# W casts on GpSimd, sorted x cleared by three engines at the start, batch 1 turned in other PSUM banks

## The chip, the core and the metric

The kernel runs on one core of one Trainium2 chip. The metric is the device time of one execution in microseconds (us): the median of three runs, lower is better. A core has five engines that run side by side[...]: TensorE (PE in the profile, its weight loads as PEld), VectorE (DVE), ScalarE (ACT), GpSimd (POOL) and SyncE (SP), which here issues the loads. Sixteen DMA engines move data between memory and the on-chip buffer.

## What is computed

Eight batches of 576 tokens go through a linear attention with eight heads of width 64. The result is one row of 512 numbers for each of 4608 tokens. It then passes a mixture of experts in which each token goes to one expert:

```python
q_s = softmax(q, axis=-1); k_s = softmax(k, axis=2)      # over the tokens
kv  = einsum('bhsd,bhse->bhde', k_s, v)                  # 64 x 64 per head
x   = einsum('bhsd,bhde->bhse', q_s, kv)                 # -> (4608, 512)

logits = x @ w_gate + modality_bias[modality_id]         # 8 experts, 2 modalities
e_idx  = argmax(logits)
gate_w = softmax(logits)[e_idx]
out[mask_e] = gate_w * (relu(x[mask_e] @ w1[e]) @ w2[e]) # w1: 512 x 1024, w2: 1024 x 512
```

The bias of a modality is large against the rest, so that all tokens of a modality go to one expert. The kernel uses this: it takes two experts from the biases, loads only their weights, and sorts each batch's tokens to the left or to the right end of a buffer `xs`, one expert each. Where the data doesn't fit this picture, a general path at the end computes all experts again. On this draw it is not entered.

## The kernel before

For each batch `attend(b)` computes kv, turns q (`tp_ps`, `et`) and the gate logits; `route(b)` finds each token's expert and its place, computes x (`x_ps`), scales it (`x_sb`), and multiplies it with a permutation, so that tokens come out sorted and turned (`xT_ps`); ScalarE writes them into `xs` twice, left and right. `slots(b)` and `places(b)` build the lists of row numbers by which the results are stored. The FFN is cut into pieces: a piece of the first layer is eight matmuls of 256 columns and a relu into `hT`, one of the second is four matmuls of 512 columns; `mains(n)` issues n pieces. Each function is a generator, and the program order on every engine is the order in which the generators are advanced. A `yield` carries a weight, and `weave` issues pieces in proportion to it.

```python
    stage = ctx.enter_context(tc.tile_pool(name="stage", bufs=6))   # loads of k, v, q, W
    ka = ... bufs=2 (PSUM);  mm = ... bufs=2;  ff = ... bufs=3;  sp_ps = ... bufs=1
    ...
    xs = persist.tile([P, KD, NSLOT], BF16)          # 128 x 4 x 4864
    lst = persist.tile([P, 3, NSL], FP32)
    nc.gpsimd.memset(lst, 0.0)
    xs_w = {}

    def clear(b):
        lo, hi = S * b, min(S * (b + 1), NSLOT // 2)
        xs_w[b] = [
            nc.gpsimd.memset(xs[:, :, c : c + hi - lo].bitcast(FP32), 0.0) for c in (lo, NSLOT - hi)
        ]

    clear(0)
    clear(1)
    ...
    def prep(b, v_eng):          # exp of k and q on ScalarE, cast of v on v_eng
    def attend(b):
        ...
        tps, tag = (ff, "ff") if b == 0 else (mm, "mm")   # banks in which q is turned
        ...
    def x_tile(b, t):
        x_ps = mm.tile([P, 512], FP32, name="x_ps", tag="mm")
    ...
    def route(b):
        ...                      # logits, max, expert: lg, mx, eqm, kk, isa, na, pos on VectorE
        nc.scalar.activation(out=lg, in_=lg, func=ACT.Exp)
        ...
        xps = [x_tile(b, 0)]
        yield 1.6
        xps.append(x_tile(b, 1))
        yield 2.4
        nc.tensor.matmul(out=r_ps[:, 0, :], lhsT=tri, rhs=isa, start=True, stop=True)
        ...                      # gsum, qi, aoff, aoff_i, pos, perm on VectorE
        scale(0)                 # x_sb of tile 0
        yield 5
        scale(1)
        free[0] = nc.vector
        for t in range(NT):      # five tiles of 64 or 128 tokens
            ...                  # xT_ps: four matmuls; x_tile(b, t + 2)
            for side, off in (("a", 0), ("b", right)):
                w = nc.scalar.copy(out=window(a + off, b, T, off > 0), in_=xT_ps[:, :, 0:T])
                if t == 0:
                    after(w, xs_w.pop(b, ()), "tokens come to cleared places")
            yield 1.2 if t < NT - 1 else 1.3
            if t + 2 < NT:
                scale(t + 2)
    ...
    def slots(b):                # VectorE: slot, hi, lo, hhi, hlo;  GpSimd: hv
    def places(b):               # TensorE: id_ps;  VectorE: lst, idb, ab, sel
```

Of the kernel before, what the change touches and what calls it, by code (L numbers as in the profile page):

```python
# [20 lines left out]
P = 128  # L21
# [21 lines left out]
def kernel(  # L43
# [67 lines left out]
    def load_batch(b, names="kvq", halves=""):  # L111
        for nm in names:
            src = {"k": k, "v": v, "q": q}[nm]

            t = stage.tile([P, HG, NJ * Dh], FP32, name="st", tag="st")
            n = HG // 2 if nm in halves else HG
            for g in range(0, HG, n):
                nc.sync.dma_start(
                    out=t[:, g : g + n, :],
                    in_=bass.AP(  # L120
                        tensor=src.tensor,
                        offset=src.offset + (b * H + 2 * g) * S * Dh,
                        ap=[[NJ * Dh, P], [2 * S * Dh, n], [1, NJ * Dh]],
                    ),
                )
            st[nm, b] = t
# [67 lines left out]
    def token_ids():  # L194
        nc.vector.tensor_scalar(out=idh_i, in0=id_i, scalar1=7, scalar2=None, op0=ALU.logical_shift_right)
        nc.vector.tensor_scalar(out=idl_i, in0=id_i, scalar1=127, scalar2=None, op0=ALU.bitwise_and)
        nc.vector.tensor_copy(out=vals[:, :, :, 0], in_=idh_i)
        nc.vector.tensor_copy(out=vals[:, :, :, 1], in_=idl_i)
# [20 lines left out]
    xs = persist.tile([P, KD, NSLOT], BF16)  # L219
    lst = persist.tile([P, 3, NSL], FP32)  # L220
    nc.gpsimd.memset(lst, 0.0)
    xs_w = {}

    def clear(b):

        lo, hi = S * b, min(S * (b + 1), NSLOT // 2)
        xs_w[b] = [
            nc.gpsimd.memset(xs[:, :, c : c + hi - lo].bitcast(FP32), 0.0) for c in (lo, NSLOT - hi)
        ]

    clear(0)
    clear(1)
    aoff_i = persist.tile([1, B * NT], I32)

    krow = persist.tile([P, NSL], FP32)
# [5 lines left out]
    eid_i = const.tile([1, 2], I32)  # L241
    bsel = const.tile([P, B * NT, E], FP32)
    modf = const.tile([P, B, NT], FP32)
    nc.vector.memset(modf, 0.0)

    def gating():

# [59 lines left out]
        nc.vector.tensor_copy(out=view(modf, [[1, NT - 1], [NT, B]], 1), in_=m_ps[:, 1:NT, :])  # L307
        nc.vector.tensor_copy(out=modf[0:64, :, 0], in_=m_ps[0:64, 0, :])

    def bias_of_tokens():  # L310
        biasd = const.tile([P, E], FP32, name="biasd")
        nc.vector.tensor_sub(out=biasd, in0=bias_b[:, 1, :], in1=bias_b[:, 0, :])
        nc.vector.tensor_tensor(
            out=bsel, in0=view(modf, [[1, B * NT], [0, E]]), in1=view(biasd, [[0, B * NT], [1, E]]), op=ALU.mult
        )
        nc.vector.tensor_tensor(
            out=bsel, in0=bsel, in1=view(bias_b, [[0, B * NT], [1, E]]), op=ALU.add
        )
# [29 lines left out]
    def after(ins, befores, why):  # L348
        for before in befores:
            tc.add_manual_dep(  # L350
                ins.ins,
                before.ins.name,
                mybir.DependencyInfo(mybir.DependencyClass.Sync, mybir.DependencyReason.DATA),
                reason=why,
            )
# [27 lines left out]
    def attend(b):  # L383

        kvbd, gx, et, vb = kvbd_b[b % 2], gx_b[b % 2], et_b[b % 2], vb_b[b % 2]
        ek, eq = eks[b], eqs[b]
        tps, tag = (ff, "ff") if b == 0 else (mm, "mm")
        kv = [ka.tile([P, 512], FP32, name="kv_ps", tag="ka") for _ in range(2)]
        for hp in range(2):
            for j in range(NJ):  # L390
# [68 lines left out]
        else:  # L459
# [4 lines left out]
                if nj > 1:  # L464
                    yield 1.2 if c0 == 0 else 2
            kvT = kv_turned()
        yield 3
        g_ps = sp_ps.tile([P, NP, E], FP32, name="g_ps", tag="sp")
        for p_ in range(NP):
            nc.tensor.matmul(  # L470
# [67 lines left out]
    def route(b):  # L538
# [38 lines left out]
        def scale(t):  # L577
            T = tsz[t]
            x_out[t] = mid.tile([P, D], BF16, name="x_sb")
            nc.vector.tensor_tensor(  # L580
                out=view(x_out[t], [[2 * Dh, HG], [Dh, 2], [1, Dh]], 0, (0, T)),
                in0=view(xps[t], [[2 * Dh, HG], [Dh, 2], [1, Dh]], 0, (0, T)),
                in1=view(qi, [[1, HG], [HG, 2], [0, Dh]], t * H, (0, T)),
                op=ALU.mult,
            )
# [21 lines left out]
            skip_runtime_bounds_check_because=WHY,  # L607
        )[1]
        scale(0)
        yield 5  # L610
        scale(1)
        free[0] = nc.vector
        for t in range(NT):
            T = tsz[t]
            xT_ps = (ka if b else ff).tile([P, KD, P], FP32, name="xT_ps", tag="ka" if b else "ff")
            for kd in range(KD):
                nc.tensor.matmul(  # L617
                    out=xT_ps[:, kd, 0:T],
                    lhsT=x_out[t][0:T, kd * P : (kd + 1) * P],
                    rhs=perm[0:T, t, 0:T],  # L620
                    start=True,
                    stop=True,
                )
            if t + 2 < NT:
                xps.append(x_tile(b, t + 2))
            right = NSLOT - (b * S + cum[t])
            for side, off in (("a", 0), ("b", right)):
                a = nc.s_assert_within(at[t], 0, b * S + cum[t] - T, skip_runtime_bounds_check_because=WHY)
                w = nc.scalar.copy(out=window(a + off, b, T, off > 0), in_=xT_ps[:, :, 0:T])  # L629
                if t == 0:  # L630
                    after(w, xs_w.pop(b, ()), "tokens come to cleared places")
            yield 1.2 if t < NT - 1 else 1.3
            if t + 2 < NT:
                scale(t + 2)
        free[0] = nc.scalar
# [203 lines left out]
    def alone(*sides):  # L839
        for side in sides:  # L840
            for _ in side:
                pass
# [11 lines left out]
    load_weights(eids[1], 1, nc.sync)  # L854
    for b in range(2, B):
        load_batch(b)
    def steps(side, n):
        for _ in range(n):
            next(side)
# [6 lines left out]
    biases()  # L866
    steps(a0, 2)
    steps(p0, 2)
    bias_of_tokens()
    alone(a0)  # L870
    steps(p1, 2)
# [5 lines left out]
    steps(r0, 1)  # L877
    a1 = attend(1)
    steps(a1, 4)
    token_ids()  # L880
    cast_weights(0, 0, nc.gpsimd)

    for _ in range(NT - 1):
        steps(r0, 1)
        steps(a1, 1)
    alone(r0)
    cast_weights(0, 1, nc.scalar)
    alone(a1)
    mains(1)
    r1 = route(1)  # L890
    cast_weights(0, 2, nc.scalar)
    steps(r1, 1)
    mains(1)
    cast_weights(0, 3, nc.scalar)
    steps(r1, 1)
    mains(2)
    steps(r1, 1)
    slots(0)
    cast_weights(1, 0, nc.gpsimd)
    for b in range(2, 5):  # L900
        clear(b)
    mains(1)
    places(0)
    mains(1)
    weave([next(r1)], 0.6)
    cast_weights(1, 1, nc.vector)
    weave(r1, 0.6)
    cast_weights(1, 2, nc.scalar)
    cast_weights(1, 3, nc.scalar)
    mains(12 - now[0])  # L910
    slots(1)
    p2 = prep(2, nc.gpsimd)
    for i in range(6):
        mains(1)
# [5 lines left out]
    def batch(b):  # L920
        side = chain(attend(b), route(b))
        for i, x in enumerate(side):
            if i == 3 and b > 2:
                slots(b - 1)
            if i == 6 and b > 2:
                places(b - 1)
            yield x

    for b in range(2, B):
        weave(batch(b), (14 if b == 2 else 15.5) / 28.6, prep(b + 1, nc.gpsimd) if b + 1 < B else (), 4)  # L930

    big = persist.tile([1, 2], I32)
    isb = persist.tile([1, 1], FP32)
# [77 lines left out]
    with tc.For_i(0, nr) as e:  # L1011
        kcol = small.tile([P, 1], FP32, name="kcol")
        first = nc.vector.tensor_copy(out=kcol, in_=view(wrow, [[1, 1]], e))
        after(first, stored, "rows are stored again")
        for part in range(4):
            dst = W[:, 0, part * 2 * F : (part + 1) * 2 * F]
            if part < 2:
                nc.gpsimd.dma_start(
                    out=view(dst, [[F, 2], [1, F]]),
                    in_=bass.AP(  # L1020
                        tensor=moe_w1.tensor,
                        offset=e * (D * F) + part * 2 * P * F,
                        ap=[[F, P], [P * F, 2], [1, F]],
                    ),
                )
            else:
                nc.gpsimd.dma_start(
                    out=view(dst, [[D, 4], [1, D]]),
                    in_=bass.AP(
                        tensor=moe_w2.tensor,  # L1030
                        offset=e * (F * D) + (part - 2) * 4 * P * D,
                        ap=[[D, P], [P * D, 4], [1, D]],
                    ),
                )
        sel1 = small.tile([P, NSL], FP32, name="sel1")
        nc.vector.tensor_scalar(out=sel1, in0=lst[:, 2, :], scalar1=kcol, scalar2=None, op0=ALU.is_equal)
        nc.vector.scalar_tensor_tensor(
            out=sel1, in0=idb, scalar=-OOB, in1=sel1, op0=ALU.add, op1=ALU.mult
        )
        for _, _, lo, w in passes:  # L1040
            hT = hbuf.tile([P, KF, GW], BF16, name="hT")
            alone(ffn1(xs[:, :, lo : lo + w], w, weights_of(0)[0], hT))
            alone(ffn2(w, weights_of(0)[1], hT, lambda: rows_of(sel1, lo, w), "stores again"))


# [28 lines left out]
```

The softmax here doesn't subtract the row's maximum and nothing guards it: scores larger than these inputs give would overflow.

## Time and profile before

| what | value |
|---|---|
| median of three runs | 267.23 us (265.94 to 267.35) |
| span of the profiled execution | 265.6 us |
| TensorE busy | 200.6 us, 76% |
| VectorE busy | 151.4 us, 57% |
| ScalarE busy | 153.8 us, 58% |
| GpSimd busy | 78.7 us, 30% |
| read from memory, written | 36.75 MB, 9.70 MB |

A row of the profile's list of stages has the stretch, its length, the busy time of each engine with the number of instructions, the clock granted to TensorE as a share of its full speed, the busy share of the DMA engines, and GB/s. A row of the list of waits reads "engine, what it was about to do, its line <- the engine and the work that ended last before it": total us, times, longest. A row of the timeline has start, duration, engine, line, operation, output <- input with shapes, and how many in a row; neighbours of a kind are merged. The duration on VectorE includes time in which an instruction has been issued and can't run.

### The profile page before, as it was taken

The numbers are of one execution on the slowest core, as the hardware profiler recorded it, in microseconds if no ns is written. First come the engines' busy times: TensorE is split into PE (matmuls) and PEld (weight loads), VectorE is DVE, ScalarE is ACT, GpSimd is POOL, SyncE is SP. The second block draws the span as 40 slices with busy tenths as digits, with TensorE's granted clock in tenths as the row PEclk, the third lists the DMA queues.
The fourth block names the chain that finished last, engine by engine and source line by source line (L and its number), as shares of the span: only waits on it lengthen the run. The fifth ranks groups of instructions, "written<-read, shape, count | busy, mean of one in ns | idle before, by whom it ended". The sixth has DMA issues, their size and how long they took to land. (4 is left out here: it accounts for less than half of the span.)

```text
span 265.6 us, 5231 instructions
## 1 busy us (share of the span) xinstructions
PE 200.6 (76%) x1934; PEld 137.4 (52%) x1954; DVE 151.4 (57%) x501; ACT 153.8 (58%) x241; POOL 78.7 (30%) x94
## 2 busy tenths in 40 slices
PE   0465668447898978898797899888788979999900
PEld 0354545135666447545565575566456637676500
DVE  7488573783043848876793967579385855311110
ACT  2977378138798559666666777665744634443300
POOL 8301000765114216022602341180142052141410
PEclk9995557759799999999999999999999999999975
DMA  6999999566999942861774010210102003030210
GB/s 233 371 390 404 393 391 321 200 206 234 356 389 343 355 174 50 346 237 64 238 246 172 2 79 0 81 79 2 42 12 111 0 39 121 0 158 2 110 57 1
DMA packets 18940, 46.58 MB, mean 175 GB/s; under 512 B 1229, under 2 KB 1229, under 8 KB 18910
## 3 DMA queue, kind: packets, MB, share of 16 engines
q1 hardware_dynamic: 15920, 36.70, 38.9%
q0 software_dynamic: 2960, 9.44, 8.8%
q8 instruction: 17, 0.28, 0.4%
q14 instruction: 13, 0.11, 0.1%
q10 hardware_dynamic: 30, 0.05, 0.1%
HBM read 36.75 MB, written 9.70 MB: 175 GB/s over the span
## 5 line engine op out<-in xcount | busy, mean ns | idle before, releaser
L726 PE MATMUL h_ps<-xs,W 128*128 128x256 bf16 x576 | 74.2, 282 | 4.7 <-ACT hT L737 2.7
L744 PE MATMUL y_ps<-W,hT 128*128 128x512 bf16 x268 | 68.9, 386 | 1.3 <-issue 0.3
L757 POOL DMA_INDIRECT out_dram<-y_sb,ix x37 | 36.7, 991 | 111.9 <-DVE y_sb L358 29.9
L726 PEld LDWEIGHTS <-W 128*128 128x128 bf16 x576 | 55.7, 101 | 14.3 <-issue 3.6
L737 ACT ACTIVATE hT<-h_ps 128x512 bf16<-128x512 f32 x73 | 42.0, 596 | 21.1 <-PE h_ps L726 20.3
L629 ACT CAST xs<-xT_ps 128x512 f32 (+2 forms) x80 | 38.8, 563 | 13.6 <-PE xT_ps L617 13.3
L744 PEld LDWEIGHTS <-hT 128*128 128x128 bf16 x296 | 26.9, 98 | 25.2 <-issue 1.1
L358 ACT COPY y_sb<-y_ps 128x512 f32<-128x512 f32 x22 | 12.9, 586 | 43.2 <-PE y_ps L744 40.9
L580 DVE TENSOR_TENSOR x_sb<-x_ps,qi 128x512 bf16<-128x512 f32 (+1 forms) x40 | 29.8, 764 | 1.2 <-PE x_ps L509 0.5
L358 DVE COPY y_sb<-y_ps 128x512 f32<-128x512 f32 x15 | 10.4, 692 | 33.0 <-PE y_ps L744 33.0
L659 POOL TENSOR_TENSOR hv<-hhi,vals 128x570 bf16<-128x570 bf16 x8 | 12.5, 1568 | 46.3 <-DVE hhi L655 42.5
L617 PE MATMUL xT_ps<-perm,x_sb 128*128 128x128 bf16 (+1 forms) x160 | 16.6, 232 | 9.2 <-DVE x_sb L580 6.6
L617 PEld LDWEIGHTS <-x_sb 128*128 128x128 bf16 (+1 forms) x160 | 10.9, 106 | 19.3 <-DVE x_sb L580 15.2
L376 ACT ACTIVATE ek<-st 128x1152 bf16<-128x1152 f32 x16 | 18.6, 1172 | 1.6 <-DMA st<-in_k_dram 1.6
L376 ACT ACTIVATE eq<-st 128x1152 bf16<-128x1152 f32 x16 | 18.4, 1158 | 0.6 <-DMA st<-in_q_dram 0.6
L509 PE MATMUL x_ps<-kvbd,et 128*128 128x128 bf16 (+1 forms) x160 | 17.5, 239 | 0.4 <-DVE et L358 0.4
L393 PE MATMUL kv_ps<-vb,ek 64*128 64x129 bf16 x288 | 12.8, 239 | 5.9 <-DVE vb L358 2.8
L429 PE MATMUL tp_ps<-ident,eq 128*128 128x128 bf16 x144 | 13.6, 241 | 4.1 <-DVE x_sb L580 2.4
L429 PEld LDWEIGHTS <-eq 128*128 128x128 bf16 x144 | 11.3, 109 | 9.1 <-issue 5.9
L393 PEld LDWEIGHTS <-ek 64*128 64x128 bf16 x288 | 10.3, 104 | 9.7 <-issue 7.6
L358 POOL CAST vb<-st 128x1152 bf16<-128x1152 f32 x12 | 13.5, 1152 | 0.0
L509 PEld LDWEIGHTS <-et 128*128 128x128 bf16 (+1 forms) x160 | 11.8, 109 | 3.3 <-issue 2.2
(148 smaller groups left out, 217.4 us busy)
## 6 DMA issues: line engine op xcount, KB each, us to landing
st<-in_k_dram SPq DMA_DIRECT2D x8, 1152.0 KB, 5.9
st<-in_moe_w_dram SPq DMA_DIRECT2D x8, 1024.0 KB, 12.6
st<-in_v_dram SPq DMA_DIRECT2D x7, 1152.0 KB, 6.3
st<-in_q_dram SPq DMA_DIRECT2D x6, 1152.0 KB, 5.7
st<-in_q_dram SPq DMA_DIRECT2D x4, 576.0 KB, 12.9
st<-in_v_dram SPq DMA_DIRECT2D x2, 576.0 KB, 8.1
out_dram<-y_sb,ix POOLq DMA_INDIRECT x37, 2.8
W<-in_moe_modality_id_dram ACTq DMA_DIRECT2D x1, 36.0 KB
```

Of the source, the lines that this page charges most:

```text
L358: return (nc.scalar.copy if eng is nc.scalar else eng.tensor_copy)(out=out, in_=in_)
L376: nc.scalar.activation(out=view((eks if nm == "k" else eqs)[b], [[Dh, 2], [HG * Dh, NJ], [1, Dh]], 2 * g * Dh), in_=src[:, 2 * g : 2 * g + ...
L393: nc.tensor.matmul(out=kv[hg][:, 130 * hp : 130 * hp + 129], lhsT=ek[rows, j, P * hp : P * hp + P], rhs=vb[rows, j, hp, 0:129], start=(j = ...
L429: nc.tensor.transpose(out=view(tp[c0], [[2 * nj * 64, 2], [1, 64]], hp * nj * 64 + jj * 64), in_=eq[:, c0 + jj, P * hp : P * hp + P], iden ...
L509: nc.tensor.matmul(out=view(x_ps, [[2 * Dh, 2], [1, Dh]], (4 * (p_ % 2) + p_ // 2) * Dh, (0, T)), lhsT=et[:, p_, tcol[t] : tcol[t] + T], r ...
L580: nc.vector.tensor_tensor(out=view(x_out[t], [[2 * Dh, HG], [Dh, 2], [1, Dh]], 0, (0, T)), in0=view(xps[t], [[2 * Dh, HG], [Dh, 2], [1, Dh ...
L617: nc.tensor.matmul(out=xT_ps[:, kd, 0:T], lhsT=x_out[t][0:T, kd * P : (kd + 1) * P], rhs=perm[0:T, t, 0:T], start=True, stop=True,)
L629: w = nc.scalar.copy(out=window(a + off, b, T, off > 0), in_=xT_ps[:, :, 0:T])
L726: nc.tensor.matmul(out=h_ps[:, f * w : (f + 1) * w], lhsT=w1(kd * F + (f0 + f) * P, P), rhs=x_in[:, kd, :], start=(kd == 0), stop=(kd == K ...
L737: nc.scalar.activation(out=h_out, in_=h_in, func=ACT.Relu)
L744: nc.tensor.matmul(out=y_ps, lhsT=hT[:, kf, t * P : (t + 1) * P], rhs=w2(kf * D, D), start=(kf == 0), stop=(kf == KF - 1),)
L757: store = nc.gpsimd.indirect_dma_start(out=out, out_offset=bass.IndirectOffsetOnAxis(ap=ix[:, t : t + 1], axis=0), in_=y_sb, in_offset=Non ...
```

## The change

It moves work between engines and in program order; the matmuls of the main path are the same.

- `xs` is cleared at the start, in four rows of 2432 words of four bytes: two rows on GpSimd, one on ScalarE (as a copy of a zero), one on VectorE. The clears of single batches go, and so do those that ran between batch 0 and batch 2.
- Of the eight parts of W (parts 0 to 3 of the first expert, 4 to 7 of the second), six are cast by GpSimd and two by ScalarE. Before, GpSimd cast two, ScalarE five and VectorE one.
- Batch 1's q is turned in the three FFN banks and no longer in the two banks that it shares with `x_ps`.
- Token ids, `slots(0)`, `slots(1)`, `places` and part of the bias work move in the order; `scale(1)` comes ahead of its yield; some weights differ, and batch 2 is woven with 12 pieces in place of 14.
- The general path becomes a loop over passes inside the loop over experts, in place of a written-out list.

```diff
-    xs_w = {}
-    def clear(b): ...
-    clear(0)
-    clear(1)
+    xs_w = [nc.gpsimd.memset(xs[:, kd, :].bitcast(FP32), 0.0) for kd in (2, 3)]
...
     nc.vector.memset(modf, 0.0)
+    xs_w.append(nc.scalar.copy(out=xs[:, 0, :].bitcast(FP32), in_=view(modf, [[0, NSLOT // 2]])))
...                            # biasd and the product with modf move from bias_of_tokens() to biases()
-        tps, tag = (ff, "ff") if b == 0 else (mm, "mm")
+        tps, tag = (ff, "ff") if b < 2 else (mm, "mm")
...
-        yield 3
+        yield 2.6
         g_ps = sp_ps.tile([P, NP, E], FP32, name="g_ps", tag="sp")
...
         scale(0)
-        yield 5
         scale(1)
+        yield 4.2
...
-                if t == 0:
-                    after(w, xs_w.pop(b, ()), "tokens come to cleared places")
-            yield 1.2 if t < NT - 1 else 1.3
+                if b == 0 and t == 0:
+                    after(w, xs_w, "tokens come to cleared places")
+            yield 1.4 if t < NT - 1 else 2
...
     for b in range(2, B):
         load_batch(b)
+    xs_w.append(nc.vector.memset(xs[:, 1, :].bitcast(FP32), 0.0))
...
     steps(p0, 2)
+    steps(a0, 2)
     bias_of_tokens()
     alone(a0)
...
     a1 = attend(1)
     steps(a1, 4)
+    cast_weights(0, 0, nc.gpsimd)
+    cast_weights(0, 1, nc.gpsimd)
+    steps(r0, 2)
+    ...                        # r0 and a1 in turn
+    alone(r0)
     token_ids()
-    cast_weights(0, 0, nc.gpsimd)
-    for _ in range(NT - 1):
-        steps(r0, 1)
-        steps(a1, 1)
-    alone(r0)
-    cast_weights(0, 1, nc.scalar)
+    slots(0)
+    steps(a1, 1)
     alone(a1)
+    cast_weights(0, 2, nc.scalar)
     mains(1)
     r1 = route(1)
-    cast_weights(0, 2, nc.scalar)
     steps(r1, 1)
-    mains(1)
+    mains(2)
     cast_weights(0, 3, nc.scalar)
     steps(r1, 1)
-    mains(2)
-    steps(r1, 1)
-    slots(0)
-    cast_weights(1, 0, nc.gpsimd)
-    for b in range(2, 5):
-        clear(b)
-    mains(1)
     places(0)
     mains(1)
-    weave([next(r1)], 0.6)
-    cast_weights(1, 1, nc.vector)
-    weave(r1, 0.6)
-    cast_weights(1, 2, nc.scalar)
-    cast_weights(1, 3, nc.scalar)
-    mains(12 - now[0])
+    cast_weights(1, 0, nc.gpsimd)
+    cast_weights(1, 1, nc.gpsimd)
+    steps(r1, 1)
+    mains(2)
+    cast_weights(1, 2, nc.gpsimd)
+    cast_weights(1, 3, nc.gpsimd)
+    weave(r1, 0.8)
     slots(1)
+    mains(14 - now[0])
...
-            if i == 6 and b > 2:
+            if i == 7 and b > 2:
                 places(b - 1)
...
-        weave(batch(b), (14 if b == 2 else 15.5) / 28.6, ...)
+        weave(batch(b), (12 if b == 2 else 15.5) / 28.9, ...)
...                            # general path:
-        for _, _, lo, w in passes:
+        with tc.For_i(0, NSL, GW // P) as at:
+            ...
```

More of the change, by code (lines that the diff above doesn't have):

```diff
@@ L221 @@
     nc.gpsimd.memset(lst, 0.0)
-    xs_w = {}
[L224 to L229, printed above, removed]
-    clear(0)
-    clear(1)
+    xs_w = [nc.gpsimd.memset(xs[:, kd, :].bitcast(FP32), 0.0) for kd in (2, 3)]
     aoff_i = persist.tile([1, B * NT], I32)
@@ L243 @@
     modf = const.tile([P, B, NT], FP32)
+    biasd = const.tile([P, E], FP32)
     nc.vector.memset(modf, 0.0)
+    xs_w.append(nc.scalar.copy(out=xs[:, 0, :].bitcast(FP32), in_=view(modf, [[0, NSLOT // 2]])))
     def gating():
@@ L308, in biases @@
         nc.vector.tensor_copy(out=modf[0:64, :, 0], in_=m_ps[0:64, 0, :])
-    def bias_of_tokens():
-        biasd = const.tile([P, E], FP32, name="biasd")
         nc.vector.tensor_sub(out=biasd, in0=bias_b[:, 1, :], in1=bias_b[:, 0, :])
@@ L315, in bias_of_tokens @@
         )
+    def bias_of_tokens():
         nc.vector.tensor_tensor(
@@ L879 @@
     steps(a1, 4)
-    token_ids()
-    cast_weights(0, 0, nc.gpsimd)
-    for _ in range(NT - 1):
-        steps(r0, 1)
-        steps(a1, 1)
-    alone(r0)
-    cast_weights(0, 1, nc.scalar)
+    cast_weights(0, 0, nc.gpsimd)
+    cast_weights(0, 1, nc.gpsimd)
+    steps(r0, 2)
+    steps(a1, 1)
+    steps(r0, 1)
+    steps(a1, 1)
+    steps(r0, 1)
+    steps(a1, 1)
+    alone(r0)
+    token_ids()
+    slots(0)
+    steps(a1, 1)
     alone(a1)
+    cast_weights(0, 2, nc.scalar)
     mains(1)
     r1 = route(1)
-    cast_weights(0, 2, nc.scalar)
     steps(r1, 1)
-    mains(1)
+    mains(2)
     cast_weights(0, 3, nc.scalar)
     steps(r1, 1)
-    mains(2)
-    steps(r1, 1)
-    slots(0)
-    cast_weights(1, 0, nc.gpsimd)
-    for b in range(2, 5):
-        clear(b)
-    mains(1)
     places(0)
     mains(1)
-    weave([next(r1)], 0.6)
-    cast_weights(1, 1, nc.vector)
-    weave(r1, 0.6)
-    cast_weights(1, 2, nc.scalar)
-    cast_weights(1, 3, nc.scalar)
-    mains(12 - now[0])
+    cast_weights(1, 0, nc.gpsimd)
[5 more added lines that the diff above has]
+    weave(r1, 0.8)
     slots(1)
+    mains(14 - now[0])
     p2 = prep(2, nc.gpsimd)
@@ L929 @@
     for b in range(2, B):
-        weave(batch(b), (14 if b == 2 else 15.5) / 28.6, prep(b + 1, nc.gpsimd) if b + 1 < B else (), 4)
+        weave(batch(b), (12 if b == 2 else 15.5) / 28.9, prep(b + 1, nc.gpsimd) if b + 1 < B else (), 4)
     big = persist.tile([1, 2], I32)
@@ L1039 @@
         )
-        for _, _, lo, w in passes:
+        with tc.For_i(0, NSL, GW // P) as at:
+            x_in = hbuf.tile([P, KF, GW], BF16, name="hT")[:, 0:KD, :]
+            nc.vector.tensor_copy(out=x_in, in_=xs[:, :, ds(at * P, GW)])
+            sel2 = small.tile([P, GW // P], FP32, name="sel2")
+            nc.vector.tensor_copy(out=sel2, in_=sel1[:, ds(at, GW // P)])
             hT = hbuf.tile([P, KF, GW], BF16, name="hT")
-            alone(ffn1(xs[:, :, lo : lo + w], w, weights_of(0)[0], hT))
-            alone(ffn2(w, weights_of(0)[1], hT, lambda: rows_of(sel1, lo, w), "stores again"))
+            alone(ffn1(x_in, GW, weights_of(0)[0], hT))
+            alone(ffn2(GW, weights_of(0)[1], hT, lambda: rows_of(sel2, 0, GW), "stores again"))
 _INS = ['q', 'k', 'v', 'moe_modality_id', 'moe_w_gate', 'moe_modality_bias', 'moe_w1', 'moe_w2']
```

## Prediction

> **What bounds the kernel now.** I read the page's row of slices first, then busy time by stage, then what TensorE waited for in the poor stages, then the timeline there. The slices:
>
> ```profile
> PE   0465668447898978898797899888788979999900
> ...
> PEclk9995557759799999999999999999999999999975
> DMA  6999999566999942861774010210102003030210
> ```
>
> One digit is 6.64 us. From slice 11 (73 us) TensorE is at 7 to 9 tenths at full clock until its work ends near 252 us. Before that it is at 4 to 6 tenths, often at half clock, while the loads keep the DMA engines full up to 44 us. By stage, where the times are us from the start:
>
> ```profile
> core 0: us, PE busy (x) PEld busy (x) DVE busy (x) ACT busy (x) POOL busy (x), PEclk, DMA share, GB/s
> 28.00:35.00 7.00, 5.75 (x50) 4.84 (x50) 3.42 (x8) 4.28 (x8) 0.00 (x0) 0.50 1.05 399
> 44.00:50.00 6.00, 1.85 (x15) 1.06 (x14) 3.67 (x13) 1.42 (x3) 1.90 (x2) 1.00 0.98 375
> 50.00:62.00 12.00, 7.88 (x51) 4.45 (x51) 8.73 (x11) 4.30 (x9) 7.27 (x8) 0.57 0.60 186
> 62.00:75.00 13.00, 10.26 (x74) 7.75 (x74) 3.21 (x14) 11.06 (x16) 4.71 (x4) 0.87 0.84 299
> 75.00:115.00 40.00, 34.23 (x377) 23.10 (x378) 26.60 (x88) 28.50 (x45) 12.01 (x11) 1.00 0.75 266
> 228.00:253.00 25.00, 24.32 (x167) 15.01 (x167) 3.55 (x9) 8.91 (x15) 7.79 (x8) 1.00 0.18 72
> ```
>
> From 75 us TensorE is 86% busy, and 97% in the final stage. So the end is set by when TensorE gets through a fixed list of matmuls; what can be won lies before 75 us. TensorE's waits between 36 and 75 us:
>
> ```profile
> PE xT_ps L617 <- DVE x_sb L580: 4.1, 2, 3.5
> PE id_ps L676 <- POOL hv L659: 4.1, 1, 4.1
> PE h_ps L726 <- ACT hT L737: 2.7, 1, 2.7
> PE h_ps L726 <- ACT W L358: 1.7, 1, 1.7
> ```
>
> That is 12.6 us in five waits. Each has its cause in the timeline. `id_ps` (places) waits since slots(0) stands on VectorE behind route(1)'s chain. `hT` comes late since two W casts (3.71 us) sit in front of it on ScalarE; the fourth wait is a W cast on ScalarE itself. The first is this:
>
> ```profile
> 51.52 4.56 POOL L228 MEMSET xs<- 128x1152 f32 x6
> ...
> 52.01 4.09 DVE L690 TENSOR_SCALAR ix<-sel 128x2 int32<-128x2 f32 x1
> ...
> 52.09 4.02 DVE L580 TENSOR_TENSOR x_sb<-x_ps,qi 128x512 bf16<-128x512 f32 x1
> ...
> 128.08 2.56 DVE L681 SCALAR_TENSOR_TENSOR idb<-lst 128x38 f32<-128x38 f32 x1
> ...
> 128.35 2.24 POOL L358 CAST vb<-st 128x1152 bf16<-128x1152 f32 x2
> ```
>
> A VectorE operation on two numbers takes 4.09 us because six clears run on GpSimd; much later one of 0.2 us takes 2.56 us beside two GpSimd casts. It gets in only when the whole row of GpSimd work is over.
>
> **What the Trainium skill says.** "SBUF — State Buffer", section "Who interferes with whom": VectorE and GpSimd share one port pair, and the loser blocks for the whole instruction of the other; two-port copies, casts and tensor_scalar collide with any GpSimd work, two-SBUF-input operations with GpSimd operations that read, PSUM sources with at most one SBUF input do not. The trace agrees: 4.09 us and 2.56 us above, while kvbd from PSUM (25.40 us, 1.20 us for four) ran undisturbed beside a GpSimd W cast. "VectorE: DVE Perf Modes", section "Zero memsets can be issued as uint32 (trn2)": a memset takes one cycle per element. The trace has 0.272 us for 256 words, so 2432 words should take about 2.6 us. "TensorE: Matmul & The Clock Gate", section "What's actually happening": the clock halves after an idle window of about 3.4 us and returns after a busy one. The trace agrees roughly: eight h matmuls took 1.85 us at clock 0.5 and 1.04 us at 1.0.
>
> **The change, part by part.**
>
> 1. *Clearing at the start.* GpSimd clears two rows of 2432 words; 1.056 us for 1152 and 0.309 for 256 give 0.83 ns a word, so 2.1 us each, 4.9 to 9.1 us: as now, in two long pieces. The two small casts of the bias (now 1.26 and 0.90 us, blocked) wait for both, to about 9.1. Then b_ps, bias_b, key and krow end near 9.9 instead of 8.0, and VectorE's own clear takes 2.6 us, to 12.4. The cast of v, which now starts at 9.10, starts near 12.4. ScalarE's copy of 2432 words (0.84 ns each by its casts of 1152 and 2048, so 2.2 us) ends at 7.0 instead of letting ek start at 6.37; ek, the gate weights and mbf slip 0.7 us, which is hidden behind v. TensorE's second kv half ends near 16.6 instead of 13.4. The bias addition moved off the path returns some 0.3 us. Batch 0's chain: **+3.0 us**.
>
> 2. *W casts on GpSimd.* The first W part lands at 25.27 whatever the chain does, since the DMA engines are full. Two casts of 1.89 us hold the port to about 29.1. Now the chain reaches x_sb(0) at 24.34, before the casts; shifted by 3 us, its two-input and tensor_scalar operations (gsum, qi, aoff_i, perm) fall into them. If they get in between the two casts, x_sb(0) starts near 29; if blocked through both, near 31. I take 30.5: **+3.2 us more**.
>
> 3. *Batch 1's turning in FFN banks, token ids and slots moved.* From x_sb(0) to the end of the first FFN group (eight h matmuls) now takes 24.34 to 39.62 = 15.3 us: x_sb(1) behind kvbd and the token ids, the turns waiting for banks of x_ps, then W part 1 on ScalarE. Afterwards VectorE does x_sb ×5 (3.4), kinv and kvbd (1.6), et (1.0), token ids (0.6), slots (2.2) and gx (0.4), 9.2 us in all; lg_ps adds 0.7 and the first group at half clock 1.9; with 0.6 for joints 12.4 us. **−2.9 us**: the first group ends at 42.9, 3.3 us later than now.
>
> 4. *From there to 20 FFN pieces* (a piece is eight h or four y matmuls). TensorE's program order shows 18 pieces ahead of batch 2's kv now and 20 afterwards. Now kv(2) starts at 75.6; two pieces of 1.04 us more make 77.7 comparable, 38.1 us after the first group's end. Afterwards the list is 19 pieces × 1.04 = 19.8, five xT and five x_ps (4.2), two id_ps (1.0), about 1 us for a cold beginning: 26 us if nothing waits. All five waits above go: slots(0) is done early, the six clears are gone, and of the eight W parts (0 to 7) parts 1, 6 and 7 leave ScalarE and part 5 VectorE. W parts 4 and 5 on GpSimd block route(1)'s lg to isa until about 14.4 us after x_sb(0), but r_ps has 7 us of h groups in front of it. ScalarE has 23 us of work in the stage (two W casts 3.8, hT 7, ten xs 5.5, y_sb 2.4, four exponentials 4.7), so I add 2.5 us of waits: 28.5. kv(2) then starts at 71.4: **6.3 us earlier with two more pieces counted in**.
>
> 5. *Batches 2 to 7.* Pieces per batch: 12 against 14 in batch 2, so total and remainder are the same. The periods now are 20.5 us for batch 2 (75.6 to 96.1), then 23.8, 24.7, 22.0 and 24.3. Batches 3 to 6 have 15.5 × 1.04 + 5.2 = 21.3 us of TensorE work, so 2.4 us are idle in each. places moves behind gx, so the blocked idb (2.56 us) no longer delays gx and lg_ps (waits of 0.9 us). scale(1) comes ahead of a yield, so xT waits less. I count 0.4 us for each of five batches: **−2 us**.
>
> 6. *General path.* It is not executed on this draw: the trace goes from the branch at 253.27 us to the end. Smaller code, no time.
>
> Sum: 267.2 − 6.3 − 2.0 = **259 us**.
>
> **Rivals.**
> - *The start eats the gain.* For it: steps 1 and 2 delay the first group by 6 us, and if W parts 4 and 5 block route(1) into the h groups, some 3 us more go. Against it: removed waits are larger than that. Time 264 to 268.
> - *ScalarE or arrival of the loads sets the middle.* 23 us of work in 28 leave little room, and DMA engines are full to 44 us. But W part 7 is now issued only at 38.09, when ScalarE frees part 1's buffer; with a GpSimd cast that is near 29 us, so the later loads come earlier. Time 261 to 264 if ScalarE binds.
> - *The start costs little.* If the port lets VectorE in between GpSimd instructions (the two bias casts at 4.69 and 6.08 us each waited for one clear only), or the first W casts land late, x_sb(0) is near 28 and the clock is warm sooner: 251 to 255.
> - *Gain given back later.* TensorE's idle share of 14% after 75 us could grow, as GpSimd's stores and casts lie differently. Nothing in the profile speaks for more than 1 to 2 us.
>
> **Range and chances.** Steps 1 and 2 are uncertain by 3 us, step 4 by 4, step 5 by 3: together about 6 us to each side for eight in ten, 252.5 to 265.5. Two per cent faster is 261.9 or less, inside the upper half of the range. Slower by 2% would need every blocked wait and none of the removed ones.
>
> **What would show it.** Step 1: v's cast near 12.4 us and VectorE's clear near 2.6 us. Step 2: x_sb(0) between 29 and 31 us, and single VectorE operations of over 1 us beside the W casts. Step 3: first h group complete near 43. Step 4: no wait of id_ps on hv, no wait over 2 us of xT on x_sb, kv(2) near 71. Step 5: periods of about 23 us. Wrong at once if kv(2) starts after 75 us, or if TensorE's share from there to the end drops below 84%.

## Result and the profile after

The changed kernel takes 252.06 us (median of four runs, 250.34 to 252.15) against 267.08 us: ratio 0.943, 95% interval 0.938 to 0.948. The prediction was 259.0 us with a range of 252.5 to 265.5, so the gain was undersized by almost half. The profiled spans are 250.5 and 265.6 us, 15.1 us apart.

The page's slices of the changed kernel (6.26 us each):

```profile
PE   0084669899776888797989788986998789999950
...
PEclk9999997999997999999999999999999999999996
...
DMA  6999999999999419632962101120112003021120
```

TensorE is at 6 to 9 tenths from slice 4 (25 us) until its work ends; before, such a level came for good with slice 9 (60 us), and the full clock with slice 11 (73 us). The DMA engines are full until about 80 us, in place of 44: the loads of batches 2 and 3 follow the weights without a pause. By stage:

```profile
core 0: us, PE busy (x) PEld busy (x) DVE busy (x) ACT busy (x) POOL busy (x), PEclk, DMA share, GB/s
28.00:35.00 7.00, 5.34 (x50) 4.88 (x51) 6.11 (x17) 4.14 (x9) 2.08 (x1) 1.00 1.04 398
44.00:50.00 6.00, 5.22 (x42) 2.67 (x40) 4.29 (x15) 4.48 (x7) 1.26 (x2) 1.00 1.05 391
50.00:62.00 12.00, 11.89 (x101) 8.50 (x98) 8.27 (x20) 9.00 (x15) 7.86 (x6) 1.00 1.03 385
62.00:75.00 13.00, 10.41 (x136) 7.44 (x134) 5.93 (x22) 9.01 (x14) 4.84 (x5) 1.00 1.01 375
75.00:115.00 40.00, 33.26 (x347) 22.47 (x348) 25.83 (x88) 25.06 (x43) 11.01 (x11) 0.96 0.57 206
213.00:237.50 24.50, 24.50 (x189) 17.00 (x188) 5.54 (x16) 11.12 (x19) 5.84 (x6) 1.00 0.17 66
```

From 44 to 62 us TensorE is busy 17.1 of 18 us, before 9.7. From 75 to 115 us it is busy 33.3 of 40 us, before 34.2. The waits of TensorE between 36 and 75 us:

```profile
PE g_ps L463 <- ACT kvT L440: 2.9, 2, 1.7
PE kv_ps L386 <- POOL vb L351: 0.8, 1, 0.8
PE lg_ps L472 <- DVE gx L467: 0.8, 1, 0.8
PE y_ps L737 <- ACT W L351: 0.5, 1, 0.5
PE xT_ps L610 <- DVE x_sb L573: 0.3, 1, 0.3
```

That is 5.3 us in place of 12.6, and no wait for hv or for a relu is left. The two kernels side by side, in us; kv(b) is the first kv matmul of batch b, and a piece counts as 0.9, which is explained below:

| point | before | after | moved by |
|---|---|---|---|
| first cast of v starts | 9.10 | 12.33 | +3.2 |
| x_sb(0) starts | 24.34 | 28.53 | +4.2 |
| first FFN group complete | 39.6 | 40.1 | +0.5 |
| 20 pieces done, kv(2) starts | 75.6 with 18, so 77.4 | 62.2 | −15.2 |
| last matmul ends | 252.5 | 241.5 | −11.0 |
| end of the span | 265.6 | 250.5 | −15.1 |

So the start loses, the middle gains 15.7 us, the stretch from batch 2 on loses 4.2 us again, and the end, where no matmul runs, gains 4.1.

### The profile page after: what moved, and what is told of

The parts are those of the page before. It is cut to its first block, busy times and chain, and to the rows that moved or that the text cites. A ratio compares the mean times of both kernels' runs of the same rounds, so it can differ in the third digit from the quotient of the medians.

```text
span 250.5 us, 5251 instructions
## 1 busy us (share of the span) xinstructions
PE 195.6 (78%) x1954; PEld 136.0 (54%) x1954; DVE 155.7 (62%) x507; ACT 147.9 (59%) x233; POOL 81.8 (33%) x90
## 3 DMA queue, kind: packets, MB, share of 16 engines
q1 hardware_dynamic: 15920, 36.70, 40.1%
## 5 line engine op out<-in xcount | busy, mean ns | idle before, releaser
L737 PE MATMUL y_ps<-W,hT 128*128 128x512 bf16 x288 | 71.8, 384 | 0.6 <-ACT W L351 0.5
L719 PE MATMUL h_ps<-xs,W 128*128 128x256 bf16 x576 | 70.9, 275 | 0.1
L719 PEld LDWEIGHTS <-W 128*128 128x128 bf16 x576 | 54.6, 99 | 7.2 <-issue 0.5
L730 ACT ACTIVATE hT<-h_ps 128x512 bf16<-128x512 f32 x69 | 40.4, 597 | 26.7 <-PE h_ps L719 24.9
L622 ACT CAST xs<-xT_ps 128x512 f32 (+2 forms) x80 | 39.4, 555 | 14.4 <-PE xT_ps L610 13.7
L351 DVE COPY y_sb<-y_ps 128x512 f32<-128x512 f32 x17 | 11.8, 692 | 36.8 <-PE y_ps L737 34.0
L351 ACT COPY y_sb<-y_ps 128x512 f32<-128x512 f32 x20 | 11.7, 585 | 31.1 <-PE y_ps L737 27.8
L573 DVE TENSOR_TENSOR x_sb<-x_ps,qi 128x512 bf16<-128x512 f32 (+1 forms) x40 | 26.3, 681 | 1.9 <-PE x_ps L502 1.2
L610 PE MATMUL xT_ps<-perm,x_sb 128*128 128x128 bf16 (+1 forms) x160 | 15.8, 225 | 12.8 <-DVE x_sb L573 8.8
L351 POOL CAST W<-st 128x2048 bf16<-128x2048 f32 x6 | 11.4, 1922 | 17.3 <-ACT vb L351 16.3
```

Of the source, the lines that this page charges most:

```text
L351: return (nc.scalar.copy if eng is nc.scalar else eng.tensor_copy)(out=out, in_=in_)
L573: nc.vector.tensor_tensor(out=view(x_out[t], [[2 * Dh, HG], [Dh, 2], [1, Dh]], 0, (0, T)), in0=view(xps[t], [[2 * Dh, HG], [Dh, 2], [1, Dh ...
L610: nc.tensor.matmul(out=xT_ps[:, kd, 0:T], lhsT=x_out[t][0:T, kd * P : (kd + 1) * P], rhs=perm[0:T, t, 0:T], start=True, stop=True,)
L719: nc.tensor.matmul(out=h_ps[:, f * w : (f + 1) * w], lhsT=w1(kd * F + (f0 + f) * P, P), rhs=x_in[:, kd, :], start=(kd == 0), stop=(kd == K ...
L730: nc.scalar.activation(out=h_out, in_=h_in, func=ACT.Relu)
L737: nc.tensor.matmul(out=y_ps, lhsT=hT[:, kf, t * P : (t + 1) * P], rhs=w2(kf * D, D), start=(kf == 0), stop=(kf == KF - 1),)
```

## Experiments

Each experiment ran beside the kernel before, in one of three groups; ratios are to it. In the first two, `before` took 264.3 us, in the third 266.6 us, so times of different groups are compared through their ratios, and shifts within a trace are used for stages. In the third group the changed kernel itself gave 251.24 us, ratio 0.940 (0.936 to 0.945).

> The changed kernel itself, as the base of the other runs on this chip: ratio to the kernel before 0.94, as measured.

In the first two groups the profile of `u_path`, which has the changed kernel's main path, serves as reference: kv(2) at 62.3 us, kv(3) at 86.5, last matmul ending at 239.3.

### The general path, written out or as loops

```diff
 # u_path: the changed kernel; d_path: the kernel before with the reverse edit
-        with tc.For_i(0, NSL, GW // P) as at:
-            ...
+        for _, _, lo, w in passes:
+            ...
```

> The changed kernel with the general path written out again; it is not entered. Theory 1: its length costs about 4 us between the last matmul and the end (13.1 us before, 9.0 us in the changed kernel), so this run takes about 256 us, and all else in the trace stays. Rival: the end is shorter for another reason (order of the last stores, when they land), and this run takes 252 us with 9 us at the end.

> The kernel before with only the nested loops of the general path. Theory 1: about 263 us, 9 us from the last matmul to the end. Rival: 267 us, 13 us.

Measured: u_path 253.98 us, ratio 0.960 (0.956 to 0.964); d_path 260.96 us, ratio 0.987 (0.983 to 0.991). From the last matmul's end to the end of the span it is 13.2 us in u_path and 9.0 in d_path; 13.1 before, 9.0 after. The events at the branch around the general path, as the answer on that line gives them (least/median/most ns, first to last start in us), in u_path:

```profile
L1007 POOLq EVENT_SEMAPHORE  x16: 17/43/43, 243.2 to 248.3; - x16
...
L1007 SPq EVENT_SEMAPHORE  x12: 28/28/28, 244.4 to 245.2; - x12
...
L1007 PEldq COMPARE_BRANCH  x3: 97/193/3973, 236.0 to 245.8; - x3
...
L1007 POOLq COMPARE_BRANCH  x3: 38/41/45, 240.8 to 248.4; - x3
```

and in the changed kernel:

```profile
L1007 POOLq EVENT_SEMAPHORE  x15: 17/43/547, 243.2 to 246.3; - x15
...
L1007 SPq EVENT_SEMAPHORE  x12: 28/28/1087, 244.3 to 246.1; - x12
...
L1007 PEldq COMPARE_BRANCH  x3: 101/179/319, 238.1 to 246.7; - x3
...
L1007 POOLq COMPARE_BRANCH  x3: 38/38/50, 243.1 to 246.4; - x3
```

With the long code one branch on TensorE takes 3.97 us; it starts at 239.5 us, just behind the last matmul. GpSimd stands still behind its own branches: the first starts at 240.8 us and its next semaphore event comes at 243.2, and 2.8 us pass behind the second. It passes its last wait at 248.3 us, 3.1 us after SyncE's. With the loops the branch on TensorE takes 0.32 us, GpSimd goes on less than 0.1 and 0.4 us behind its branches, and it passes its last wait 0.2 us after SyncE's. Theory 1 holds: in both kernels the written-out code, which is never entered, cost 4.1 to 4.2 us between the last matmul and the end; in the median of d_path 3.4 us of it are seen (264.36 against 260.96). Why an engine stands still behind such a branch isn't shown, nor whether the length of the code or another trait of its written-out form decides.

### 14 pieces woven into batch 2

```diff
-        weave(batch(b), (12 if b == 2 else 15.5) / 28.9, ...)
+        weave(batch(b), (14 if b == 2 else 15.5) / 28.9, ...)
```

> The changed kernel with 14 FFN pieces woven into batch 2 in place of 12. Theory 2: with 12 pieces TensorE runs out of work between r_ps and the first xT of batch 2, idles 2 us and goes to the half clock; with 14 the period of batch 2 (24.3 us) doesn't grow, or shrinks to 21 to 22, and the end comes 2 to 4 us earlier: 248 to 250 us. Rival: batch 2 is slow because exponentials and casts of v come late; then two more pieces lengthen it by 1.8 us and the time stays at 252 us.

Measured: 249.6 us, ratio 0.9446 (0.941 to 0.948). Against 253.98 − 4.2 = 249.8 us, an estimate from u_path for the changed kernel on that chip, nothing is gained. But it isn't the rival's picture either: batch 2 shrank from 24.2 to 21.6 us and batch 3 grew from 23.4 to 25.9. The program order tells why. Both orders have 32 pieces issued when kv(3) begins: `mains` issues only pieces whose batch is sorted, and the two sorted batches have no more. A higher rate uses the same 12 pieces sooner, and TensorE runs dry at the end of batch 2 instead of in its middle: it waits 1.2 and 1.1 us for `xs` there, and kv(3)'s 35 matmuls then take 2.00 us, in u_path 1.18. The expectation had overlooked this limit. From it comes theory 5, tested below.

### Clears at the start behind the cast of v

```diff
-    xs_w = [nc.gpsimd.memset(xs[:, kd, :].bitcast(FP32), 0.0) for kd in (2, 3)]
-    xs_w.append(nc.scalar.copy(out=xs[:, 0, :]...)); xs_w.append(nc.vector.memset(xs[:, 1, :]...))
+    # after steps(p0, 4): all four rows on GpSimd, the first waits for batch 0's second cast of v
+    xs_w = [nc.gpsimd.memset(xs[:, kd, :].bitcast(FP32), 0.0) for kd in range(KD)]
```

> The changed kernel with all four rows of xs cleared by GpSimd, begun only when batch 0's v has been cast, none on VectorE and ScalarE. Theory 3: the clears at the start delay batch 0's chain by 3 us, and this reaches the end: v's cast at 9.1 us again, x_sb(0) near 25, first FFN group 2 to 3 us earlier, 249 to 250 us. Rival: the W parts (second landed at 28.3 us, cast until 30.4) and their casts hold the first FFN group, so that it comes at most 1 us earlier: 251 to 252 us.

Measured: 246.27 us, ratio 0.932 (0.929 to 0.936). GpSimd had been idle from 9.1 to 25.3 us in the changed kernel; the timeline of gstart by engine (GpSimd, VectorE, TensorE), with start and duration in us and, in brackets, the idle time before and what ended it:

```profile
11.20 8.32 POOL L856 MEMSET xs<- 128x2432 f32 x4 [6.28 <-DVE vb L350]
25.33 1.89 POOL L350 CAST W<-st 128x2048 bf16<-128x2048 f32 x1 [5.81 <-DMA st<-in_moe_w_dram]
...
8.95 0.76 DVE L350 CAST vb<-st 128x1152 bf16<-128x1152 f32 x1 [2.95 <-DMA st<-in_v_dram]
...
24.37 1.27 DVE L572 TENSOR_TENSOR x_sb<-x_ps,qi 64x512 bf16<-64x512 f32 x2
...
33.50 1.87 PE L718 MATMUL h_ps<-xs,W 128*128 128x256 bf16 x8
```

v's cast is back at 8.95, x_sb(0) at 24.4, and the first FFN group starts 4.8 us earlier than in u_path (33.5 against 38.3). kv(2) is 3.0 us earlier and the last matmul 4.7 us. Theory 3 holds: the clears at the start cost the changed kernel some 3 us that reach the end (2.2 us by the ratios 0.940 and 0.932, 3.5 against the estimate of 249.8, 4.7 by the two traces). The rival (W parts hold the first group) falls.

### The clears of before in the changed kernel, and the other way round

```diff
 # u_clear: the changed kernel                       # d_clear: the kernel before, reverse edit
+    clear(0); clear(1)                               # at the start, GpSimd, as before
...
     cast_weights(1, 1, nc.gpsimd)
+    for b in range(2, 5): clear(b)
```

> The changed kernel with the clears of before: batches 0 and 1 by GpSimd at the start, batches 2 to 4 by GpSimd behind the cast of W part 5. Theory 4 (the middle's gain is the sum of the removed waits, each about its length): 3 us gained at the start, 4 to 5 us lost in the middle where VectorE is held, TensorE cold again: 253 to 255 us. Rival (the clears cost nothing in the new order since TensorE has pieces to do meanwhile): 249 to 251 us.

> The kernel before with only the clears moved to the start on three engines. Theory 4: loses 3 us at the start, gains the wait of 3.5 us of xT and part of the cold stretch from 50 to 60 us: 262 to 266 us. Rival (the clears are the main cause of the slow middle): 258 us or less.

Measured: u_clear ratio 0.9435 (0.936 to 0.951); d_clear 263.69 us, ratio 0.9985 (0.996 to 1.001). d_clear gained nothing: its expectation, 262 to 266 of 267.1 us, is a ratio of 0.981 to 0.996, and was just missed. The trace shows what it was built on: the first group is complete at 43.8 us, 4.2 later than before, and kv(2) is at 74.7, 0.9 earlier, so start and middle cancel. The rival (258 us or less) falls. u_clear's two fast executions took 247.58 and 250.71 us and its profile is of a slower one, so only its stages are read: x_sb(0) is at 23.9, and then VectorE is held in route(1), as its timeline and GpSimd's show:

```profile
40.81 4.57 POOL L229 MEMSET xs<- 128x1152 f32 x6
...
41.79 3.62 DVE L574 TENSOR_SCALAR gsum<-gsum 128x5 f32<-128x5 f32 x1
```

One tensor_scalar of 0.17 us takes 3.62 us beside the six clears, and TensorE's wait of xT for x_sb is 4.7 us. kv(2) comes at 64.2. By time, u_clear can't be told from the changed kernel, and its interval holds a part of both theory 4's range (253 to 255 us, a ratio of 0.947 to 0.955) and the rival's (0.932 to 0.940). The rival's reason falls, as TensorE does wait. As arranged, moving the clears is no gain that these runs show: the wait in the middle is traded for one at the start.

### The W casts on the engines of before

```diff
-    cast_weights(0, 1, nc.gpsimd)     # parts 1; 5; 6 and 7
+    cast_weights(0, 1, nc.scalar)     # behind route(0)
...
-    cast_weights(1, 1, nc.gpsimd)
+    cast_weights(1, 1, nc.vector)
-    cast_weights(1, 2, nc.gpsimd); cast_weights(1, 3, nc.gpsimd); weave(r1, 0.8)
+    weave(r1, 0.8); cast_weights(1, 2, nc.scalar); cast_weights(1, 3, nc.scalar)
```

> The changed kernel with the W casts on the engines of before: part 1 on ScalarE, part 5 on VectorE, parts 6 and 7 on ScalarE behind route(1). Theory 4: the waits for ScalarE's casts come back (1.7 and 2.7 us), and the loads behind part 7 come later: 255 to 257 us. Rival (casts are hidden wherever they are): 252 us.

Measured: 255.38 us, ratio 0.964 (0.959 to 0.969), kv(2) at 68.2 us (+5.9 against u_path) and the last matmul ending at 244.8 (+5.5). The rival falls, and the size is at theory 4's upper edge. The named waits of TensorE for casts and relus have only 0.6 and 0.9 us in it; the rest is in a longer wait of xT for x_sb in route(1) (1.9 us against 0.3) and in matmuls at a cold clock: behind the wait for W two h pieces took 3.60 us, in the changed kernel 2.25, and behind the one for x_sb four x_ps matmuls took 0.63 us, there 0.40. So the size was right, and the two waits that were to come back are the smaller part of it.

### Batch 1's turning in the banks of x_ps

```diff
-        tps, tag = (ff, "ff") if b < 2 else (mm, "mm")
+        tps, tag = (ff, "ff") if b == 0 else (mm, "mm")
```

> The changed kernel with batch 1's q turned in the two banks that x_ps uses. Theory 4: the stretch from x_sb(0) to the end of the first FFN group grows from 11.6 us by 1 to 2 us, as the turns wait for x_sb(1): 253 to 254 us. Rival: that stretch is held by ScalarE and VectorE anyway: 252 us.

Measured: 251.1 us, ratio 0.951 (0.948 to 0.953). The first group starts at 39.8 us (+1.5), kv(2) is at 64.0 (+1.7), but the last matmul ends at 239.3 us, as in u_path. The stretch grew as theory 4 had it, and the ratio lies where theory 4 put it (253 to 254 of 267.1 us is 0.947 to 0.951). Against the estimate of 249.8 us 1.3 us are left; the profiled execution, 1.2 us below the median, shows none of it. So what the banks cost at the end, 0 to 1.3 us, stays open.

### slots(0) and places(0) behind route(1)

```diff
     token_ids()
-    slots(0)
...
-    places(0); mains(1)
-    cast_weights(1, 0, nc.gpsimd); cast_weights(1, 1, nc.gpsimd)
-    steps(r1, 1); mains(2)
+    mains(1); steps(r1, 1)
+    slots(0)
+    cast_weights(1, 0, nc.gpsimd); cast_weights(1, 1, nc.gpsimd)
+    mains(1); places(0); mains(1)
```

> The changed kernel with slots(0) and places(0) back behind route(1)'s third step, as before. Theory 4: TensorE waits again for hv (4.1 us before), and the W casts 4 and 5 come behind it on GpSimd; kv(2) 4 to 6 us later, and so is the end. Rival (r_ps and the x_sb wait take over, since route(1)'s chain on VectorE is freed by 2.4 us): kv(2) at most 2 us later.

Measured: 257.64 us against 251.24 on the same chip, ratio 0.966 (0.962 to 0.969). TensorE's timeline in u_slots:

```profile
43.72 1.02 PE L737 MATMUL y_ps<-W,hT 128*128 128x512 bf16 x4
49.44 0.74 PE L669 MATMUL id_ps<-hv,hlo 64*128 64x114 bf16 x5 [4.70 <-POOL hv L652]
49.98 1.91 PE L737 MATMUL y_ps<-W,hT 128*128 128x512 bf16 x4
```

TensorE waits 4.70 us for hv, and the four y matmuls behind it take 1.91 us in place of 1.02: the clock is cold. kv(2) is at 68.5 (+6.0), the last matmul 5.8 us later. Theory 4 holds, and the one wait cost more than its length.

### Fewer pieces ahead of batch 2

```diff
 # on top of gstart; stock18, and stock16 with two pieces less again
-    mains(14 - now[0])
+    mains(12 - now[0])
...
-        weave(batch(b), (12 if b == 2 else 15.5) / 28.9, ...)
+        weave(batch(b), (14 if b == 2 else 15.5) / 28.9, ...)
```

> The kernel of gstart with 18 instead of 20 FFN pieces ahead of batch 2's kv and 14 woven into batch 2 (32 by its end in both: there are no more before batch 2 is sorted). Theory 5: batch 2's own chain (kv to sorted tokens, 21 to 24 us) bounds that stretch, as TensorE has only 12 pieces left for it; beginning it two pieces earlier brings everything behind it 1.5 to 2 us forward. Rival (kv(2) is held by the exponentials and v's cast, not by the pieces ahead of it): no difference to gstart, ratio 0.932.

> As stock18 with 16 pieces ahead of kv(2) and 16 woven into batch 2. Theory 5: 3 to 4 us earlier than gstart at kv(3), ratio 0.918 to 0.922, if the exponentials keep up. Rival: as stock18, no difference to gstart, or later, as ScalarE has to do four exponentials beside four relus.

Measured: stock18 245.48 us, ratio 0.921 (0.917 to 0.925); stock16 247.68 us, ratio 0.928 (0.923 to 0.932). In stock18 kv(2) is at 57.9 us and kv(3) at 79.2, 2.7 us ahead of gstart's 81.9. Busy times of that stretch, batch 2's kv to batch 3's, first in the changed kernel, with the columns of the table by stage above:

```profile
62.10:86.40 24.30, 18.57 (x189) 11.75 (x188) 12.31 (x40) 15.40 (x26) 7.67 (x8) 0.93 0.93 348
```

then in gstart:

```profile
59.30:81.86 22.56, 16.72 (x187) 11.00 (x188) 12.30 (x40) 15.33 (x26) 7.58 (x8) 1.00 1.05 397
```

and in stock18:

```profile
57.80:79.20 21.40, 18.60 (x198) 11.67 (x198) 12.60 (x43) 15.94 (x27) 7.18 (x7) 1.00 1.05 396
```

The stretch takes 24.3, 22.6 and 21.4 us; stock18 puts 14 pieces into its own, the others 12. Theory 5 holds for two pieces. In stock16 kv(2) comes at 57.2 us only, 0.6 earlier instead of 1.8, and kv(3) at 80.9. TensorE's timeline there:

```profile
55.92 0.52 PE L668 MATMUL id_ps<-hv,hlo 64*128 64x114 bf16 x5 [1.11 <-POOL hv L651]
56.27 1.04 PE L718 MATMUL h_ps<-xs,W 128*128 128x256 bf16 x8
57.24 0.68 PE L385 MATMUL kv_ps<-vb,ek 64*128 64x129 bf16 x18
58.10 0.69 PE L385 MATMUL kv_ps<-vb,ek 64*128 64x129 bf16 x18 [0.18 <-POOL vb L350]
```

TensorE waits 1.11 us for hv of slots(1), and kv(2) then starts right behind a piece. v's first cast, which follows hv on GpSimd, was over near 56.9 us and would have held kv(2) nearly as late. So the rival is right that something other than the pieces holds kv(2); it is hv and the cast of v behind it, not the exponentials, of which the first was over at 54.8 us and the second at 56.3. gstart and stock18 were not run on one chip; against the changed kernel on its own chip stock18 gains 5.8 us, and it is the fastest kernel here, 0.921 of the time before.

## Why the prediction was wrong, step by step

**What bounds the kernel, right.** The end is set by when TensorE gets through its list, and the gain came from ahead of 75 us, but for 4 us behind the last matmul. Three of the slices ahead of 73 us stand at 7 and 8 tenths, above the 4 to 6 read there; no step rests on that.

**Step 1, right.** v's cast began at 12.33 us (12.4 said), TensorE's second kv half ended at 16.4 (16.6). VectorE's clear took 2.08 us, not 2.6: the 0.272 us of the short memset hold a fixed part (0.06 us, an estimate from these two). The timeline of the changed kernel:

```profile
4.69 2.33 DVE L266 CAST parts<-left 1x16 bf16<-1x16 f32 x1
...
4.88 4.21 POOL L223 MEMSET xs<- 128x2432 f32 x2
...
7.14 1.96 DVE L268 CAST parts<-key 1x2 bf16<-1x2 f32 x1
...
10.33 2.08 DVE L850 MEMSET xs<- 128x2432 f32 x1 [0.45 <-issue]
12.33 1.36 DVE L351 CAST vb<-st 128x1152 bf16<-128x1152 f32 x2
```

The casts of a few numbers wait 2.33 and 1.96 us for one GpSimd clear each, which agrees with the lock in the Trainium skill, "SBUF — State Buffer", section "Who interferes with whom".

**Step 2, mechanism right, size off.** x_sb(0) came at 28.5, below the 29 to 31 given, 1.0 us late beyond step 1 and not 3.2. Only qi was held (1.72 us): the second W part landed at 28.29 us, when perm was already running (27.78 us), so only one cast was in the way.

**Step 3, right, a little too careful.** 11.6 us from x_sb(0) to the first complete group, 12.4 said.

**Step 4, the step that failed, by size.** It had 28.5 us from the first group to kv(2), 26 for the list and 2.5 of waits; measured 22.1. The term "19 pieces × 1.04" took the record of a piece, start of its first matmul to end of its last, as what a piece costs. Consecutive pieces overlap. The profile before already had it, in the last stage:

```profile
234.91 7.15 PE L726 MATMUL h_ps<-xs,W 128*128 128x256 bf16 x64
```

These are eight pieces in 7.15 us, 0.89 each. In the same way xT and x_ps cost 0.22 us each in a row of work, not 0.42. With these the list is 19 × 0.89 + 10 × 0.22 + 0.7 for two id_ps + 0.7 for the cold beginning (an x_ps and two h pieces took 2.65 us, in a full stretch 2.0) = 20.5 us, and 1.6 us of waits and joints are left of the 2.5 added. So of the 6.4 us the list made 5.5. The same 1.04 stands in step 5.

The reasons themselves were right: undone one at a time, slots(0) costs 6.0 us at kv(2), the W casts 5.9, the banks 1.7 and the clears 1.9. In the clears, start and middle are netted: in u_clear the first group is complete 5.0 us earlier (35.1 against 40.1), and from there to kv(2) it takes 29.1 us against 22.1. The four sum to 15.5 us, and the measured shift at kv(2) is 15.2; such costs need not add up, so this is no proof that nothing else counts. Several cost more than their waits. The kernel before was at half clock from 50.5 to 60.6 us, behind the wait for hv and through those for x_sb, and from 67.5 to 70.8, behind the one for hT. This doesn't enter the sum of step 4, which counted the list afresh.

**Step 5, wrong.** Two us of gain were said; 4.2 were lost between kv(2) and the last matmul, on equal pieces, nearly all in batch 2: kv(3) is only 10.6 us earlier when a piece more is counted in before. The step claimed that with 12 in place of 14 pieces "total and remainder are the same". The limit is another: when kv(3) begins, all 32 pieces of the two sorted batches are used up in the changed kernel (31 before). Having come to 20 pieces so early, TensorE has 12 left for a batch that took 20.5 us before and 21.4 to 24.3 us in the changed kernel and its variants. Its busy share from kv(2) to its last matmul is 155.4 of 179.3 us, 86.6%, before 155.9 of 176.9, 88.1%. It waits 2.0 us for x_sb and goes cold, as the changed kernel's timeline shows:

```profile
78.29 0.29 PE L610 MATMUL xT_ps<-perm,x_sb 64*128 64x64 bf16 x4 [2.01 <-DVE x_sb L573]
78.51 0.40 PE L502 MATMUL x_ps<-kvbd,et 128*128 128x128 bf16 x4
78.74 1.82 PE L737 MATMUL y_ps<-W,hT 128*128 128x512 bf16 x4
```

Four y matmuls take 1.82 us. No wait of 0.2 us or more for a load stands in that stretch. g14 shows that a higher rate doesn't help, stock18 that an earlier start of batch 2 does. How much of the loss is the small stock of pieces and how much the cold clock and the places of the pieces was not separated: with the same 12 pieces batch 2 took 24.3 us here, 22.6 in gstart and 21.6 in g14. Batches 3 to 6 gained 0.4 us together, not 0.4 each; what places behind gx and the earlier scale(1) do was not tried by themselves.

**Step 6, wrong.** "Smaller code, no time" missed 4.1 us, shown by u_path and d_path in both directions. The trace before had the sign: 13.1 us from the last matmul to the end, and a branch of 4.03 us on TensorE:

```profile
L1011 PEldq COMPARE_BRANCH  x3: 101/196/4027, 249.1 to 259.1; - x3
```

**In sum.** On equal pieces kv(2) came 8.9 us earlier than said, 6.2 us were lost again behind it, and the end gave 4.1: 6.8 of the 6.9 us by which the time was missed. That the error in the middle was not seen in full in the time is luck, as step 5 erred the other way.

Of the rivals, "the start costs little" came nearest in time. One of its conditions was met, x_sb(0) near 28 us since a W part landed late; but that is 2 us of the miss, and the start did cost 4 us. "Gain given back later" came true as well, with 4.2 us where no more than 1 to 2 were seen.

## What to carry to other kernels

Size a unit of pipelined work by the spacing of such units in a full stretch, not by the length of one record. When one stage gets faster, count what stock of work it hands to the next: TensorE reached batch 2 15 us earlier, had no more than 12 pieces left beside it, and lost 4 us there. A clear that must be somewhere goes where GpSimd is idle and VectorE has nothing that it holds, here behind the cast of v: beside the 8.3 us of clears in gstart VectorE's tensor_scalar for kinv took 0.23 us and its copies into et 0.89, as in the changed kernel. And code that is never entered can cost time at the end of a program, here 4 us.

## What the runs showed of the hardware that was not expected

The page's clock row doesn't tell how fast matmuls run ahead of the trace's first clock record, which lies at 16.3 us before and at 34.5 us in the changed kernel; until then it shows full speed. Near 30 us it has 5 tenths before and 9 in the changed kernel, yet the same four xT matmuls take the same time. The timeline of the kernel before:

```profile
29.18 0.63 PE L617 MATMUL xT_ps<-perm,x_sb 128*128 128x128 bf16 x4
```

and of the changed kernel:

```profile
29.98 0.63 PE L610 MATMUL xT_ps<-perm,x_sb 128*128 128x128 bf16 x4
```

In full stretches at a granted 1.0 they take 0.40 us, so both were cold. The time of a known matmul is the better gauge. The Trainium skill, "TensorE: Matmul & The Clock Gate", section "What's actually happening", has the clock halve after an idle window of about 3.4 us. In batch 2 of the changed kernel an idle stretch of 2.0 us was enough: the four x_ps matmuls right behind it still took 0.40 us, and the four y matmuls after them 1.82 in place of 1.02.

Whether a VectorE instruction gets the port between two GpSimd instructions differed: the two bias casts got in after one clear each (2.33 and 1.96 us), while in the kernel before a tensor_scalar waited until the last of six clears was over and a scalar_tensor_tensor for two casts. So the prediction's reading, that VectorE gets in only behind the whole row of GpSimd work, doesn't hold in general. What decides it was not tried.
